# A pre-norm linear-attention and FFN block rewritten as one ordered list of operations

## The chip, the core and the metric

The kernel runs on one core of a Trainium2 chip. TensorE (PE) multiplies matrices out of SBUF into the eight banks of PSUM, VectorE (DVE) and ScalarE (ACT) work on vectors, GpSimd (POOL) builds masks, and SyncE (SP) issues the DMAs. The metric is the time of one execution on the device in microseconds (us); smaller is better.

## The reference

The sequence has 2048 rows of 512, the attention 32 heads of 16, the FFN 1792 columns in the middle. All arrays are bf16; B_x is not used.

```python
x = A_x
h = x + _A_ref(_layernorm(x), A_wqkv, A_wo)
h2 = h + _B_ref(_layernorm(h), B_w1, B_w2)

# _A_ref: q, k, v = split heads of x @ wqkv
phi = lambda t: where(t > 0, t + 1, exp(t)) + 1e-6
kv = einsum("bhsd,bhse->bhde", phi(k), v);  z = sum over s of phi(k)
o = (phi(q) @ kv) / (phi(q) . z + 1e-6);    return o @ wo
# _B_ref: return maximum(x @ w1, 0) @ w2
```

## The kernel before

The rows are 16 tiles of 128, in four chunks of four tiles. The value projection is never made for single rows: the kernel sums `gps`, the product of the normalized rows (transposed) with phi(k), over all tiles, and multiplies by the weights of v afterwards (`kvps`), masks the blocks of the heads (`kvbd`), and multiplies by wo (`mps`, kept as `m_sb`). So the attention is one loop over the tiles for k, and then, for each chunk, phi(q) divided by its denominator (`pqs`) times `m_sb`.

Stage one, for each tile t: the statistics of LN1 on DVE (`A_S`: bn_stats into `st`, bn_aggr into `mv`), its rstd by Ln and Exp on ACT, the norm on DVE (`A_N`, into `ln`), four transposes on PE and a copy out by ACT (`A_T`, into `lnT`), the k projection (`A_K`, `kps`), phi by ACT and DVE (`phi_act`, `phi_dve`, into `pk_all`) and the sum into `gps` (`A_G`). phi takes an Exp on ACT (`e`), for some tiles a Relu on ACT (`r`), then on DVE the minimum with 1 (line 211) and either an add (215) or relu and add in one (217).

Between that and the FFN stand z (`zps`), the q projections (`q_mm`, `qps`), the denominators, and h. For the first chunk PE adds x into h with an identity matrix (`h_first`, line 468) and transposes LN2's result; for the other chunks DVE adds x (line 447), and four DMA transposes issued by SP (line 456) bring LN2's result `hn` into `lnT`. LN2's norm subtracts the mean and multiplies by rstd, so it waits for rstd.

The FFN of a chunk is 14 groups `proj_group` (`pps`, four matmuls each, relu alternately by ACT, line 484, and DVE, line 486, into `at`), then four tiles of `ffn_group` (`fps`, 14 matmuls each), whose results `ffn_out` adds to h on DVE (line 501) and SP stores. The groups of the next chunk's denominators and h are woven among the first twelve projections.

The order on each engine is the order in which the program issues its instructions; `after` and `tick` put some DVE work back by a group. PSUM has two pools of four buffers, `mm` and `acc`, and a group waits for the buffer that comes next. SP issues all DMAs in one queue, and an instruction that waits there holds back all that stand behind it.

Of the kernel before, what the change touches and what calls it, by code (L numbers as in the profile page):

```python
# [14 lines left out]

@with_exitstack
def kernel(
# [10 lines left out]

# [27 lines left out]
    wqkv_v = A_wqkv.rearrange("(k p) n -> p k n", p=P)  # L56

# [45 lines left out]
    zeros = const.tile([P, CW], BF16, name="zeros")  # L103
    ident = const.tile([P, P], BF16, name="ident")
    mask = const.tile([P, P], BF16, name="mask")
    nc.vector.memset(zeros[:], 0.0)
    nc.vector.memset(eps5[:], 1e-5)
    nc.vector.memset(eps6[:], 1e-6)
    nc.vector.memset(ones[:], 1.0)
# [40 lines left out]
    hnT_c = lnT_c  # L150
    pqT_c = [big.tile([P, KD, CW], BF16, name=f"pqT{c}") for c in range(NCH)]
# [6 lines left out]
    pk_all = big.tile([P, NT, D], BF16, name="pk_all", tag="at0")  # L158

    gps = [psum.tile([P, D], F32, name=f"gps{kd}", tag="acc") for kd in range(KD)]  # L160


    def warm(n):
        for _ in range(n):
            nc.tensor.matmul(gps[3][:], lhsT=zeros[:, 0:P], rhs=zeros[:], start=True, stop=True)

    warm(9)


    def rstd_of(mv, n):  # L170
        rstd = work.tile([P, n], F32, name="rstd", tag=f"rstd{n}", bufs=4)
        nc.scalar.activation(out=rstd[:], in_=mv[:, :, 1], func=ACT.Ln, bias=eps5[:], scale=1.0)
        nc.scalar.activation(out=rstd[:], in_=rstd[:], func=ACT.Exp, scale=-0.5)
        return rstd

    def stats(mv, k, src):
        st = work.tile([P, nc.vector.BN_STATS_DIM], F32, name="st", tag="st", bufs=4)
        nc.vector.bn_stats(out=st[:], in_=src)  # L178
        nc.vector.bn_aggr(out=mv[:, k, :], in_=st[:])  # L179

    def norm(dst, src, mv, rstd, k):
        nc.vector.tensor_scalar(  # L182
            out=dst, in0=src, scalar1=mv[:, k, 0:1], scalar2=rstd[:, k : k + 1],
            op0=ALU.subtract, op1=ALU.mult,
        )

    def transpose(src, tag="mm"):
        tp = psum.tile([P, KD * P], BF16, name="tp", tag=tag)
        for kd in range(KD):
            nc.tensor.transpose(tp[:, kd * P : (kd + 1) * P], src[:, kd * P : (kd + 1) * P], ident[:])  # L190
        return tp

    def evac_T(dst3, tp, on_act, k=KD):
        src3 = tp.rearrange("p (k n) -> p k n", k=k)
        if on_act:
            nc.scalar.activation(out=dst3, in_=src3, func=ACT.Copy)  # L196
        else:
            nc.vector.tensor_copy(out=dst3, in_=src3)

    def phi_act(ps, relu_on_act):  # L200
        e = work.tile([P, CW], BF16, name="e", tag="e", bufs=4)
        nc.scalar.activation(out=e[:], in_=ps, func=ACT.Exp)  # L202
        r = None
        if relu_on_act:
            r = work.tile([P, CW], BF16, name="r", tag="r", bufs=4)
            nc.scalar.activation(out=r[:], in_=ps, func=ACT.Relu)
        return e, r

    def phi_dve(ps, dst, er):
        e, r = er  # L210
        nc.vector.tensor_scalar(  # L211
            out=e[:], in0=e[:], scalar1=1.0, scalar2=1e-6, op0=ALU.min, op1=ALU.add
        )
        if r is not None:
            nc.vector.tensor_tensor(out=dst, in0=r[:], in1=e[:], op=ALU.add)
        else:
            nc.vector.scalar_tensor_tensor(  # L217
                out=dst, in0=ps, scalar=0.0, in1=e[:], op0=ALU.max, op1=ALU.add
            )

    def q_mm(c, jq):
        qps = psum.tile([P, CW], F32, name="qps", tag="mm")
        for kd in range(KD):
            nc.tensor.matmul(  # L224
                qps[:], lhsT=wq_sb[:, kd, jq * P : (jq + 1) * P], rhs=lnT_c[c][:, kd, :],
                start=(kd == 0), stop=(kd == KD - 1),
            )
        return qps


    later = []

    def after(n, fn):
        later.append([n, fn])

    def tick():
        due = [x for x in later if x[0] <= 0]
        later[:] = [x for x in later if x[0] > 0]
        for x in later:
# [12 lines left out]


    group_of = {0: [0], 1: [1], 2: [2], 3: [3]}
    for t in range(4, NT, 2):
        group_of[t + 1] = [t, t + 1]
    where = {t: (g, k) for g in group_of.values() for k, t in enumerate(g)}
    mvs, rstds, lns, tps, kpss, ers = {}, {}, {}, {}, {}, {}

    def A_S(t):  # L260
        g, k = where[t]
        if k == 0:
            mvs[g[0]] = work.tile(
                [P, len(g), nc.vector.BN_AGGR_DIM], F32, name="mv", tag=f"mv{len(g)}", bufs=4
            )
        stats(mvs[g[0]], k, x_nat[:, t, :])
        if k == len(g) - 1:
            rstds[g[0]] = rstd_of(mvs[g[0]], len(g))
# [344 lines left out]
```

## Time and profile before

| what | value |
|---|---|
| median of 3 runs | 181.35 us (181.35 to 181.62) |
| the profiled execution | 181.33 us |
| its span | 179.6 us |
| granted TensorE clock | 0.997 |
| PE, DVE, ACT busy in the span | 170.1, 110.3, 80.9 us |
| moved by DMA | 11.69 MB, mean 65 GB/s |

The span is the time between the first and the last recorded event of the program on the core; the 1.7 us beside it are what the execution takes around it. In the rows that follow, a group is named by its line, engine and operation, what it writes and what it reads, then the number of instructions, their busy time and the mean of one in ns. PEld is the loading of weights, which overlaps PE.

### The profile page before, as it was taken

How to read it: one execution, taken by the hardware profiler on the slowest of the kernel's cores; microseconds unless marked ns; L12 is line 12 of the kernel's file. 1: busy time of each engine (PE TensorE's matmuls, PEld its weight loads, DVE VectorE, ACT ScalarE, POOL GpSimd, SP SyncE). 2: the span in 40 equal slices, each digit the busy share in tenths (PEclk: the TensorE clock that was granted, in tenths of full speed). 3: DMA queues.
4: the chain of work that ended last, by engine and by line, in shares of the span. 5: the costliest groups of instructions: out<-in, count | busy, mean ns of one | idle time of the engine just before them, and what ended most of it. 6: DMA issues, size and time to landing. Idle time of an engine off the chain costs nothing.

```text
span 179.6 us, 2419 instructions
## 1 busy us (share of the span) xinstructions
PE 170.1 (95%) x899; PEld 79.7 (44%) x916; DVE 110.3 (61%) x247; ACT 80.9 (45%) x162; POOL 4.7 (3%) x21
## 2 busy tenths in 40 slices
PE   7888999999998899999999999999999999999991
PEld 2334555546444444444444444444444444444461
DVE  4889999556898866988132788323498613343320
ACT  3868888856874997322008722003932100331000
POOL 7300000000000000000000000000000000000000
PEclk9999999999999999999999999999999999999998
DMA  5999960000000000003400000431000250000011
GB/s 135 318 346 384 374 201 2 0 0 4 0 4 0 0 0 0 2 4 70 106 29 29 0 4 0 88 89 57 0 0 4 48 127 29 29 0 4 29 58 31
DMA packets 15627, 11.69 MB, mean 65 GB/s; under 512 B 7040, under 2 KB 15104, under 8 KB 15616
## 3 DMA queue, kind: packets, MB, share of 16 engines
q1 hardware_dynamic: 15616, 11.54, 21.3%
q8 instruction: 7, 0.11, 0.3%
q14 instruction: 4, 0.03, 0.1%
HBM read 7.86 MB, written 2.10 MB: 55 GB/s over the span
## 4 chain that ended last, share of the span: by engine, by line
PE 70%; DVE 18%; ACT 6%; issue 2%; DMA 1%; DVEq 0%
PE fps L493 22%; PE pps L479 20%; PE gps L304 7%; PE kps L297 6%; DVE st L178 5%; PE qps L224 5%; PE hps L423 5%; DVE at L486 2%; PE fpsh L493 2%; DVE hn L182 2%; DVE mv L179 2%; DVE h_nat L447 1%; ACT lden L410 1%; ACT rden L412 1%; PE tp L190 1%
## 5 line engine op out<-in xcount | busy, mean ns | idle before, releaser
L479 PE MATMUL pps<-lnT,w_sb 128*128 128x512 bf16 x220 | 53.0, 379 | 0.9 <-ACT lnT L196 0.4
L493 PE MATMUL fps<-w_sb,at 128*128 128x512 bf16 x205 | 46.1, 379 | 0.6 <-DVE at L486 0.4
L484 ACT ACTIVATE at<-pps 128x512 bf16<-128x512 f32 x28 | 16.7, 595 | 60.6 <-PE pps L479 60.6
L493 PEld LDWEIGHTS <-at 128*128 128x128 bf16 x238 | 23.1, 98 | 26.2 <-DVE at L486 1.3
L479 PEld LDWEIGHTS <-w_sb 128*128 128x128 bf16 x224 | 21.9, 98 | 27.3 <-issue 1.7
L501 DVE TENSOR_TENSOR o_t<-fps,h_nat 128x512 bf16<-128x512 f32 x15 | 10.4, 692 | 29.1 <-PE fps L493 29.1
L486 DVE TENSOR_SCALAR at<-pps 128x512 bf16<-128x512 f32 x28 | 19.1, 680 | 9.3 <-PE pps L479 9.3
L304 PE MATMUL gps<-pk_all,ln 128*128 128x512 bf16 x61 | 15.9, 379 | 0.9 <-DVE pk_all L217 0.5
L423 PE MATMUL hps<-m_sb,pqs 128*128 128x512 bf16 x63 | 16.6, 379 | 0.1
L297 PE MATMUL kps<-wk_sb,lnT 128*128 128x512 bf16 x62 | 16.2, 379 | 0.1
L224 PE MATMUL qps<-lnT,wq_sb 128*128 128x512 bf16 x62 | 15.7, 379 | 0.2
L178 DVE BATCH_NORM_STATS2 st<-x_nat 128x6 f32<-128x512 bf16 x16 | 11.0, 685 | 1.7 <-DMA x_nat<-in_A_x_dram 1.7
L211 DVE TENSOR_SCALAR e<-e 128x512 bf16<-128x512 bf16 x32 | 8.9, 278 | 4.7 <-ACT e L202 4.7
L202 ACT ACTIVATE e<-qps 128x512 bf16<-128x512 f32 x16 | 9.4, 600 | 4.6 <-PE qps L224 4.6
L178 DVE BATCH_NORM_STATS2 st<-h_nat 128x6 f32<-128x512 bf16 x16 | 11.0, 689 | 0.4
L414 DVE TENSOR_TENSOR pqs<-pqT,rden 128x512 bf16<-128x512 bf16 x12 | 5.1, 425 | 9.1 <-ACT rden L412 9.0
L202 ACT ACTIVATE e<-kps 128x512 bf16<-128x512 f32 x16 | 9.5, 596 | 2.5 <-PE kps L297 2.5
L196 ACT ACTIVATE lnT<-tp 128x512 bf16<-128x512 bf16 x17 | 10.0, 590 | 0.5 <-PE tp L190 0.5
L423 PEld LDWEIGHTS <-pqs 128*128 128x128 bf16 x64 | 6.3, 98 | 8.6 <-DVE pqs L414 1.2
L304 PEld LDWEIGHTS <-ln 128*128 128x128 bf16 x64 | 6.2, 97 | 8.4 <-issue 1.3
L224 PEld LDWEIGHTS <-wq_sb 128*128 128x128 bf16 x64 | 6.0, 98 | 7.2 <-issue 0.8
L447 DVE TENSOR_TENSOR h_nat<-hps,x_nat 128x512 bf16<-128x512 f32 x12 | 8.2, 686 | 0.9 <-PE hps L423 0.8
(72 smaller groups left out, 134.8 us busy)
## 6 DMA issues: line engine op xcount, KB each, us to landing
w_sb<-in_B_w_dram SPq DMA_DIRECT2D x2, 1792.0 KB, 14.2
out_dram<-o_t SPq DMA_DIRECT2D x15, 128.0 KB, 1.7
x_nat<-in_A_x_dram SPq DMA_DIRECT2D x2, 512.0 KB, 6.5
x_nat<-in_A_x_dram SPq DMA_DIRECT2D x4, 128.0 KB, 2.2
wk_sb<-in_A_wqkv_dram SPq DMA_DIRECT2D x2, 256.0 KB, 3.3
x_nat<-in_A_x_dram SPq DMA_DIRECT2D x2, 256.0 KB, 4.3
wq_sb<-in_A_wqkv_dram SPq DMA_DIRECT2D x1, 512.0 KB, 7.9
wv_sb<-in_A_wqkv_dram SPq DMA_DIRECT2D x1, 512.0 KB, 8.9
```

Of the source, the lines that this page charges most:

```text
L178: nc.vector.bn_stats(out=st[:], in_=src)
L196: nc.scalar.activation(out=dst3, in_=src3, func=ACT.Copy)
L202: nc.scalar.activation(out=e[:], in_=ps, func=ACT.Exp)
L224: nc.tensor.matmul(qps[:], lhsT=wq_sb[:, kd, jq * P : (jq + 1) * P], rhs=lnT_c[c][:, kd, :], start=(kd == 0), stop=(kd == KD - 1),)
L297: nc.tensor.matmul(kpss[t][:], lhsT=lnT_c[c][:, kd, j * P : (j + 1) * P], rhs=wk_sb[:, kd, :], start=(kd == 0), stop=(kd == KD - 1),)
L304: nc.tensor.matmul(gps[kd][:], lhsT=lns[t][:, kd * P : (kd + 1) * P], rhs=pk_all[:, t, :], start=(t == 0), stop=(t == NT - 1),)
L423: nc.tensor.matmul(hps[:], lhsT=pqss[c][jb][:, j * P : (j + 1) * P], rhs=m_sb[:, jb, :], start=(jb == 0), stop=(jb == KD - 1 and c > 0),)
L479: nc.tensor.matmul(pps[:], lhsT=w1_sb[:, kd, f * P : (f + 1) * P], rhs=hnT_c[c][:, kd, :], start=(kd == 0), stop=(kd == KD - 1),)
L484: nc.scalar.activation(out=acts[c][:, f, :], in_=pps[:], func=ACT.Relu)
L486: nc.vector.tensor_scalar(out=acts[c][:, f, :], in0=pps[:], scalar1=0.0, scalar2=None, op0=ALU.max)
L493: nc.tensor.matmul(fps[:], lhsT=acts[c][:, f, j * P : (j + 1) * P], rhs=w2_sb[:, f, n0:n1], start=(f == 0), stop=(f == KF - 1),)
L501: nc.vector.tensor_tensor(out=o_t[:], in0=fps[:], in1=h_nat[:, t, n0:n1], op=ALU.add)
```

## The change

The pools, `after`, `tick` and `woven` are gone. Every operation is a small function, and a table ORDER lists them in the order in which they are issued; a word is a function's name and its numbers. Upper-case letters are LN1 and k: S and A the statistics of a tile, R its rstd, N the norm, T and E (or V, on DVE) a transpose on PE and the copy out, X the transpose by DMA, K the projection, F, U, M, D the Exp, Relu, minimum and add of phi, G the sum. Lower-case ones are LN2 and the FFN: h, hD, s, a, r, n, t, e, v, x, then p (projection), pA and pD (relu on ACT or DVE), f, fo and fd. Q, qF, qU, qM, qD are the q projection and its phi, d, dl, dx, dm the denominators, lx to lo the loads. The last number of p, Q, K, h, f is the bank of PSUM, which is now one tile `bk` of eight banks; F, U, M, D, their q forms, pA, pD, gA, mA, mD and rm take a tile number and a count, and with a count of 2 they handle two banks (1024 columns) in one instruction. Tiles 0 to 3 have phi one by one.

Six things change in what is computed where. Tiles 8 to 15 of LN1 are transposed by DMA (X). The Relu of every phi is on ACT. In the first chunk DVE adds x to h (hD), and the ident matmul is gone. LN2's n only subtracts the mean; rstd, which is positive and passes through the relu, is multiplied in by fo, so n no longer waits for rstd. The loads of wq, wv, wo, w1 and w2 are in halves, in another order. LN1's rows lie in `h_nat`, and pk(t) in `pk_lo` and `acts[0]`.

```diff
+ORDER = """
+lx.0.1 lx.1.1 lx.2.1 lk.0.2 lk.2.2 lx.3.1 lx.4.2 lx.6.2 lx.8.4 lx.12.4 table const masks warm.9.7 S.0 S.1 A.0
+R.0.1 A.1 S.2 R.1.1 N.0.0.2 N.0.2.2 A.2 N.1 S.3 A.3 T.0.3.2.2 T.0.0.0.2 E.0.0.2 E.0.2.2 T.1.1 warm.1.7 E.1
...
-    lnT_c = [big.tile([P, KD, CW], BF16, name=f"lnT{c}") for c in range(NCH)]
+    ln_nat = h_nat
+    bk = psum.tile([P, 8, CW], F32, name="bk")
+    op_X = lambda t: nc.sync.dma_start_transpose(out=lnT_of(t), in_=ln_nat[:, t, :])
+    op_x = lambda t: nc.sync.dma_start_transpose(out=lnT_of(t), in_=hn[:, t % NQ, :])
...
+    def relu_of(kind, i, n):
+        nc.scalar.activation(out=buf(rb, kind, i, n), in_=bank(at_bank[kind, i], n), func=ACT.Relu)
+    def add_of(kind, i, n):
+        nc.vector.tensor_tensor(
+            out=dsts[kind](i, n), in0=buf(rb, kind, i, n), in1=buf(eb, kind, i, n), op=ALU.add
+        )
...
-        norm(hns[c, j][:], h_nat[:, c * CT + j, :], mv2[c, j0], rstd2[c, j0], j - j0)
+    def op_n(t):
+        nc.vector.tensor_scalar(
+            out=hn[:, t % NQ, :], in0=h_nat[:, t, :], scalar1=mv2[:, t, 0:1], scalar2=None,
+            op0=ALU.subtract,
+        )
...
-        nc.tensor.matmul(hps[:], lhsT=ident[:], rhs=x_nat[:, j, :], start=False, stop=True)
-        nc.scalar.activation(out=h_nat[:, j, :], in_=hps[:], func=ACT.Copy)
+    def op_hD(t, n=1):
+        nc.vector.tensor_tensor(
+            out=h_nat[:, t : t + n, :], in0=bank(at_bank["h", t], n), in1=x_nat[:, t : t + n, :],
+            op=ALU.add,
+        )
+    def op_pD(c, f, n):
+        nc.vector.tensor_scalar(
+            out=acts[c % 2][:, f : f + n, :], in0=bank(at_bank["p", c, f], n),
+            scalar1=0.0, scalar2=None, op0=ALU.max,
+        )
...
-        nc.vector.tensor_tensor(out=o_t[:], in0=fps[:], in1=h_nat[:, t, n0:n1], op=ALU.add)
-        nc.sync.dma_start(out=of_v[:, t, n0:n1], in_=o_t[:])
+    def op_fo(t, k=0, w=KD):
+        cols = slice(k * P, (k + w) * P)
+        nc.vector.scalar_tensor_tensor(
+            out=o_t[:, t % NO, cols], in0=bk[:, at_bank["f", t, k], 0 : w * P],
+            scalar=rstd2[:, t : t + 1], in1=h_nat[:, t, cols], op0=ALU.mult, op1=ALU.add,
+        )
...
+    for word in ORDER.split():
+        name, *idx = word.split(".")
+        ops[name](*map(int, idx))
```

The first place is SP's queue during LN1, after the loads of the first eight tiles. Before:

```order
L76 DMA x_nat<-in_A_x_dram 128x4x512 x2
L93 DMA wq_sb<-in_A_wqkv_dram 128x4x512
L94 DMA wv_sb<-in_A_wqkv_dram 128x4x512
L95 DMA wo_sb<-in_A_wo_dram 128x4x512
L96 DMA w_sb<-in_B_w_dram 128x4x1792
L97 DMA w_sb<-in_B_w_dram 128x14x512
```

Changed (lnT_83 and lnT_84 are the third and fourth chunk, h_nat holds LN1's rows, w_sb is w1 or w2):

```order
L198 DMA x_nat<-in_A_x_dram 128x4x512 x2
L201 DMA wv_sb<-in_A_wqkv_dram 128x2x512 x2
L201 DMA wq_sb<-in_A_wqkv_dram 128x2x512
L201 DMA w_sb<-in_B_w_dram 128x2x1792
L269 DMA_TRANSPOSE lnT_83<-h_nat 128x4x128 x4
L269 DMA_TRANSPOSE lnT_84<-h_nat 128x4x128 x2
L201 DMA wq_sb<-in_A_wqkv_dram 128x2x512
L269 DMA_TRANSPOSE lnT_84<-h_nat 128x4x128 x2
L201 DMA w_sb<-in_B_w_dram 128x7x512
L201 DMA wo_sb<-in_A_wo_dram 128x2x512
```

The transposes, each of which waits for its tile's norm on DVE, now stand ahead of half of wq, of wo and of most of the FFN weights.

The second place is DVE from kvbd to LN2 of the first chunk. Before (pqT_128 and pqT_129 are phi(q) of the first and second chunk):

```order
L367 TENSOR_TENSOR kvbd<-kvps,mask 128x512
L211 TENSOR_SCALAR e<-e 128x512
L215 TENSOR_TENSOR pqT_129<-r,e 128x512
L386 CAST m_sb<-mps 128x512 x2
L403 TENSOR_TENSOR pqs<-rps,pqT_128 128x512 x4
L211 TENSOR_SCALAR e<-e 128x512
L215 TENSOR_TENSOR pqT_129<-r,e 128x512
L211 TENSOR_SCALAR e<-e 128x512
L217 SCALAR_TENSOR_TENSOR pqT_129<-qps,e 128x512
```

Changed (pqT_85 and pqT_86 are the same two, bk is PSUM):

```order
L370 TENSOR_TENSOR kvbd<-bk,mask 128x512
L302 TENSOR_SCALAR eb<-eb 128x1024
L380 CAST m_sb<-bk 128x1024
L305 TENSOR_TENSOR pqT_86<-rb,eb 128x1024
L408 TENSOR_TENSOR pqs<-bk,pqT_85 128x1024 x2
L441 TENSOR_TENSOR h_nat<-bk,x_nat 128x512 x2
L217 BN_STATS st_101<-h_nat 128x6 x2
L218 BN_AGGR mv_102<-st_101 128x2
L441 TENSOR_TENSOR h_nat<-bk,x_nat 128x512
L236 TENSOR_SCALAR hn<-h_nat,mv_102 128x512
```

Pairs stand in place of single instructions, h of the first chunk comes to DVE, and the rest of the second chunk's phi moves behind LN2's statistics.

The third place is DVE in the FFN's projections of the second chunk, while h and LN2 of the third are made. Before:

```order
L486 TENSOR_SCALAR at<-pps 128x512
L447 TENSOR_TENSOR h_nat<-hps,x_nat 128x512
L178 BN_STATS st<-h_nat 128x6
L179 BN_AGGR mv_1293<-st 128x2
L182 TENSOR_SCALAR hn<-h_nat,mv_1293,rstd 128x512 x4
L486 TENSOR_SCALAR at<-pps 128x512
L501 TENSOR_TENSOR o_t<-fps,h_nat 128x512 x4
```

Changed (at_96 is the second chunk's buffer):

```order
L305 TENSOR_TENSOR pqT_88<-rb,eb 128x1024
L236 TENSOR_SCALAR hn<-h_nat,mv_102 128x512
L217 BN_STATS st_101<-h_nat 128x6
L218 BN_AGGR mv_102<-st_101 128x2 x2
L236 TENSOR_SCALAR hn<-h_nat,mv_102 128x512 x2
L218 BN_AGGR mv_102<-st_101 128x2
L236 TENSOR_SCALAR hn<-h_nat,mv_102 128x512
L461 TENSOR_SCALAR at_96<-bk 128x1024
L478 SCALAR_TENSOR_TENSOR gT<-bk,rstd_103,h_nat 128x512
```

Each norm follows its own tile's statistics instead of all four standing behind the chunk's rstd, and the last relu of the chunk is one instruction for two groups.

More of the change, by code (lines that the diff above doesn't have):

```diff
@@ L16 @@
+"""
 @with_exitstack
@@ L176, in stats @@
[L176 to L181, printed above, removed]
+    acts = [big.tile([P, KF, CW], BF16, name=f"at{i}") for i in range(2)]
+    pk_lo = big.tile([P, 2, D], BF16, name="pk_lo")
+    st = big.tile([P, NT, nc.vector.BN_STATS_DIM], F32, name="st")
+    mv = big.tile([P, NT, nc.vector.BN_AGGR_DIM], F32, name="mv")
@@ L254 @@
[L254 to L268, printed above, removed]
@@ L379 @@
-    rd4 = work.tile([P, CW], BF16, name="rd4", tag="rd4", bufs=1)
-    nc.scalar.activation(out=rd4[:], in_=ld4[:], func=ACT.Exp, scale=-1.0)
-    q11 = q_mm(1, 1)
-    for jb in range(KD):
-        mps = psum.tile([P, D], F32, name="mps", tag="acc")
-        nc.tensor.matmul(mps[:], lhsT=kvbd[:, jb, :], rhs=wo_sb[:, jb, :], start=True, stop=True)
-        if jb < 2:
-            nc.vector.tensor_copy(out=m_sb[:, jb, :], in_=mps[:])
-        else:
-            nc.scalar.activation(out=m_sb[:, jb, :], in_=mps[:], func=ACT.Copy)
@@ L389 @@
-    er11 = phi_act(q11[:], True)
-    pqss = [[None] * KD for _ in range(NCH)]
-    def new_pqs(c, jb):
-        pqss[c][jb] = work.tile([P, CW], BF16, name="pqs", tag="pqs", bufs=8)
-        return pqss[c][jb]
-    rpss = [psum.tile([P, CW], F32, name="rps", tag="mm" if jb < 2 else "acc") for jb in range(KD)]
-    for jb in range(KD):
-        rows = slice(jb * Q4, (jb + 1) * Q4)
-        nc.tensor.matmul(rpss[jb][:], lhsT=erep[rows, :], rhs=rd4[rows, :], start=True, stop=True)
-    for jb in range(KD):
-        pqs = new_pqs(0, jb)
-        nc.vector.tensor_tensor(out=pqs[:], in0=rpss[jb][:], in1=pqT_c[0][:, jb, :], op=ALU.mult)
@@ L418, with op_kx, op_m, op_mA @@
-    mv2, rstd2, hns = {}, {}, {}
-    def h_mm(c, j):
-        hps = psum.tile([P, D], F32, name="hps", tag="acc")
+    def op_kx():
+        kvps = bk[:, at_bank["kv"], :].rearrange("p (k n) -> p k n", k=KD)
+        nc.vector.tensor_tensor(out=kvbd[:], in0=kvps, in1=mask_b, op=ALU.mult)
+    def op_m(jb, b):
+        at_bank["m", jb] = b
+        nc.tensor.matmul(bk[:, b, :], lhsT=kvbd[:, jb, :], rhs=wo_sb[:, jb, :], start=True, stop=True)
+    def op_mA(jb, n):
+        nc.scalar.activation(out=m_sb[:, jb : jb + n, :], in_=bank(at_bank["m", jb], n), func=ACT.Copy)
@@ L422, in h_mm, with op_mD, op_d4 @@
+    def op_mD(jb, n):
+        nc.vector.tensor_copy(out=m_sb[:, jb : jb + n, :], in_=bank(at_bank["m", jb], n))
+    def op_d4(c, b):
+        at_bank["d4", c] = b
         for jb in range(KD):
             nc.tensor.matmul(
[L424 to L435 removed]
@@ L471, with op_dl4 @@
-    acts = {}
-    def proj_group(c, f):
-        if f == 0:
-            pool = big if c % 2 == 0 else work
-            acts[c] = pool.tile([P, KF, CW], BF16, name="at", tag=f"at{c % 2}", bufs=1)
-        pps = psum.tile([P, CW], F32, name="pps", tag="acc" if c == 0 and f < 4 else "mm")
+                bk[jb * Q4 : (jb + 1) * Q4, b, :], lhsT=zhd[:, jb, :], rhs=pqT[c][:, jb, :],
+                start=True, stop=True,
+            )
+    def op_dl4(c):
+        nc.scalar.activation(
+            out=ld[:, c % 2, :], in_=bk[:, at_bank["d4", c], :], func=ACT.Ln, bias=eps6[:], scale=1.0
+        )
@@ new lines, in op_dx4, with op_rp, op_rm @@
+    def op_dx4(c):
+        nc.scalar.activation(out=rd[:, c % 2, :], in_=ld[:, c % 2, :], func=ACT.Exp, scale=-1.0)
+    def op_rp(c, jb, b):
+        at_bank["rp", c, jb] = b
+        rows = slice(jb * Q4, (jb + 1) * Q4)
+        nc.tensor.matmul(
+            bk[:, b, :], lhsT=erep[rows, :], rhs=rd[rows, c % 2, :], start=True, stop=True
+        )
+    def op_rm(c, jb, n):
+        i = (c * KD + jb) % NQ
+        nc.vector.tensor_tensor(
+            out=pqs[:, i : i + n, :], in0=bank(at_bank["rp", c, jb], n), in1=pqT[c][:, jb : jb + n, :],
+            op=ALU.mult,
+        )
```

569 lines of the change are left out of this document (229 added, 340 removed).

## The prediction

> **What bounds the kernel now.** I read the page's busy shares first, then the busy time by stage, then the chain that ended last.
>
> ```profile
> span 179.6 us, 2419 instructions
> PE 170.1 (95%) x899; PEld 79.7 (44%) x916; DVE 110.3 (61%) x247; ACT 80.9 (45%) x162; POOL 4.7 (3%) x21
> GB/s 135 318 346 384 374 201 2 0 0 4 0 4 0 0 0 0 2 4 70 106 29 29 0 4 0 88 89 57 0 0 4 48 127 29 29 0 4 29 58 31
> ```
>
> PE is busy almost throughout, but a busy PE is not a full PE, so I cut the span into four stages at places where the chain changes hands (start:end, length, PE, PEld, DVE, ACT, POOL busy, granted clock, DMA share, GB/s).
>
> ```profile
> 0.00:14.47 14.47, 11.04 (x53) 4.56 (x55) 10.18 (x31) 9.27 (x23) 4.71 (x21) 1.00 0.88 272
> 14.47:47.70 33.23, 32.99 (x253) 17.66 (x257) 26.04 (x69) 25.84 (x54) 0.00 (x0) 1.00 0.34 120
> 47.70:61.12 13.42, 12.35 (x67) 5.38 (x68) 12.24 (x31) 9.42 (x21) 0.00 (x0) 1.00 0.00 1
> 61.12:176.03 114.91, 113.70 (x528) 52.11 (x537) 61.46 (x119) 36.39 (x67) 0.00 (x0) 1.00 0.12 32
> ```
>
> The chain in order of time gives the price of each kind of work when it follows its like without a gap (start, length, what).
>
> ```profile
> 2.90 0.70 DVE st L178
> ...
> 4.78 0.85 DVE ln L182 x2
> 5.63 0.61 DVE st L178
> ...
> 8.10 0.18 DVE mv L179
> 8.28 0.19 DVE e L211
> 8.56 0.43 DVE pk_all L215
> 8.99 0.35 DVE ln L182
> ...
> 14.47 1.02 PE gps L304 x4
> 15.50 0.22 PE tp L190 x4
> 15.72 0.86 PE kps L297 x4
> ...
> 41.29 1.58 PE zps L340 x64
> ...
> 45.48 0.89 PE kvps L362 x16
> 46.37 0.36 PE d L373 x4
> ...
> 49.24 2.39 DVE pqs L403 x4
> ...
> 59.11 0.49 ACT r L206
> ...
> 61.12 1.89 PE pps L479 x8
> ...
> 93.51 1.73 PE pps L479 x8
> ...
> 172.93 3.07 PE fpsh L493 x28
> 176.02 0.42 DVE o_t L501
> ```
>
> Eight 512-column matmuls cost 1.73, so one costs 0.216 and a group of four 0.865; a transpose of one tile (four pieces) 0.22; zps 1.58; kvps 0.89; d 0.36. By count the kernel has 728 matmuls of 512 columns (64 each of kps, gps, qps and hps, 4 with ident, 4 mps, 4 rps, 12 dps, 224 pps, 224 fps with the halves counted together) and 20 tile transposes: 157.4 + 4.4 + 1.58 + 0.89 + 0.36 = 164.7 us that PE must spend. Its last matmul ends at 176.0, so 11.3 us are lost to waits and the cold start. By stage: up to 14.47 PE has done 24 matmuls and five transposes, 6.3 us, and lost 8.2. From 14.47 to 47.70 it lost 0.3. From 47.70 to 61.12 the work is 12.1 and 1.3 is lost, while DVE is busy 12.24 of 13.42. From 61.12 on the work is 524 x 0.216 = 113.3 of 114.9: 1.6 lost. Thus a gain can come from fewer PE instructions, from the start, from the DVE stage, and hardly from anything else.
>
> **PE work removed.** Tiles 8 to 15 of LN1 are no longer transposed on PE: 8 x 0.22 = 1.76. The four ident matmuls that added x into h are gone: 4 x 0.216 = 0.86. PE is the bound where they stood, so 2.62 us fall out whole, to 162.1. Rows of the trace behind the remaining prices:
>
> ```profile
> L501 DVE TENSOR_TENSOR o_t<-fps,h_nat 128x512 bf16<-128x512 f32 x15 | 10.4, 692 | 29.1 <-PE fps L493 29.1
> L501 DVE TENSOR_TENSOR o_t<-fpsh,h_nat 128x256 bf16<-128x256 f32 x2 | 0.8, 424 | 1.9 <-PE fpsh L493 1.9
> L196 ACT ACTIVATE lnT<-tp 128x512 bf16<-128x512 bf16 x17 | 10.0, 590 | 0.5 <-PE tp L190 0.5
> L196 ACT ACTIVATE lnT<-tph 128x256 bf16<-128x256 bf16 x2 | 0.7, 384 | 0.1
> 81.13 5.23 SPq L456 DMA_TRANSPOSE lnT<-hn  x4
> lnT<-hn SPq DMA_TRANSPOSE x12, 2.4
> x_nat<-in_A_x_dram SPq DMA_DIRECT2D x2, 512.0 KB, 6.5
> wk_sb<-in_A_wqkv_dram SPq DMA_DIRECT2D x2, 256.0 KB, 3.3
> ```
>
> **Pairs.** 256 columns more cost DVE 268 ns, so 512 more cost 0.54; one f32 instruction after another costs 0.60 (2.39 for four), a pair 1.14 instead of 1.20. On ACT 256 more cost 206 ns, 512 more 0.41: a pair 0.90 instead of 0.98. No 1024-column row exists; the bounds are 0.60 (nothing for the second half, excluded by the slope) and 1.20 on DVE. So pairing gives each engine about 7% on these instructions, and the first half waits for the second group, 0.865 us. It is not on the path while PE is the bound. The work on ACT also falls by eight evacuations of 0.49, and rises because all feature-map relus are now there.
>
> **The start.** PE's first rows of work (the warm-up matmuls, then K.0 and K.1):
>
> ```profile
> 1.24 3.63 PE L165 MATMUL gps<-zeros 128*128 128x512 bf16 x9 [1.24 <-DVE ones L109]
> 5.92 1.03 PE L297 MATMUL kps<-wk_sb,lnT 128*128 128x512 bf16 x4
> 7.75 1.03 PE L297 MATMUL kps<-wk_sb,lnT 128*128 128x512 bf16 x4
> ```
>
> DVE now does S.0, S.1, A.0, A.1, S.2 before N.0: 2.90 + 0.70 + 0.61 + 0.18 + 0.18 + 0.61 = 5.2, two halves of N.0 to 5.7, transposes, two half evacuations on ACT, and K.0 at about 6.7, 0.8 later than its 5.9 before; K.1 then follows at once where it used to come 1.8 later. DVE feeds the rest: sixteen S, A, N at 0.61 + 0.18 + 0.35, four M and D alone (0.62), three pairs (about 0.96, my estimate between 0.62 and 1.24), the copy V.2 as 0.43: 24.0 from 2.9, with some 0.4 of waits N.15 ends at 27.3. PE from K.0 up to K.15 has fifteen K, eleven G, six transposes, 23.8 us, with some 1.5 of short waits on T.3, G.1 and G.4: K.15's turn is at 32.0. Nine more groups, 7.8, and Q.0.3 ends at 39.8.
>
> The moved transposes run beside this. SP spends 1.31 on each (5.23 for four). X.10 leaves when N.10 is done (21.65 by the same count), then X.11, X.13, X.12, the half of wq (0.5) and X.14: X.15 is issued at 28.7 and lands 2.4 later, 31.1, 0.9 ahead of its use. The loads that stood in front of them are out of the way: 4.2 MB by about 15 us at the GB/s row (40 slices of 4.49 us). Queued behind them: half of wq, issued at 27.4, needed at 32.9 (256 KB landed in 3.3); wo, needed about 45; w2 and half of w1, needed from 61: 3.2 MB at 350 GB/s after 30 is 39. Four more load issues cost SP some 0.5 each, covered by that slack. If the cover were gone, each us of lateness of X.15 is a us of the end.
>
> **The middle.** From Q.0.3's end at 39.8 to the first FFN matmul there are G.15, zps, twelve Q groups, kvps, four m, d4, four rp, sixteen h, four transposes and four d: 21.0 us. I followed the order by the prices above. The path is kx, m, then d4, its Ln and Exp on ACT, rp, the two paired products: h.0 waits 0.4 for the second. DVE then does hD, s, a, n for four tiles and the pair q.1.2; the last transposes and d.1.3 wait 0.45 for n.2 and v.3. LN2 no longer waits for rstd in front of n, which is applied in fo. So 0.85 is lost where stages two and three lost 1.6, and p.0.0 starts at 61.7. Start and middle together lose 8.6 instead of 9.7: -1.1. By then PE has done four Q groups and four d more than before at its 61.12, 4.33 us.
>
> **The FFN.** Its lost 1.6 is mostly the order on DVE (start, length, engine, line; in brackets the idle time and what ended it):
>
> ```profile
> 112.44 0.69 DVE L486 TENSOR_SCALAR at<-pps 128x512 bf16<-128x512 f32 x1
> 113.19 2.98 PE L493 MATMUL fps<-w_sb,at 128*128 128x512 bf16 x12 [0.18 <-DVE at L486]
> DVE hn L182 <- ACT rstd L173: 2.4, 4, 0.6
> ```
>
> The relu of the last group stands behind four hn, which wait for rstd. In the new order the n need no rstd and the last relus stand clear of them. A pair of banks is free 1.2 after its second group and is wanted again 1.73 after: 0.5 of slack each. In the second chunk I find n.9 ending 5.5 us ahead of p.2.3; its transpose, fourth on SP, lands 1.1 ahead. The outputs fd.0 to fd.2 now queue behind four transposes on SP; fo.4, which reuses their buffer, comes 2 to 3 us after they land. Half the loss stays, by my choice, because those margins are thin: -0.8. The tail is as it was: two halves of 256 columns, one DVE instruction of 0.42, one output.
>
> [...]
>
> **Sum.** The profiled execution took 181.33 (span 179.6 and 1.7 around it; the median is 181.35). 181.33 - 2.62 - 1.1 - 0.8 = 176.8; I add 0.2 for semaphore latencies that I left out: 177.0.
>
> **Rivals.**
> 1. Only the removed work pays: the new waits eat what the old ones cost. 181.33 - 2.62 = 178.7, 178.0 to 179.5. For it: margins of 0.4 to 1.1 at six places. Against it: DVE's path is shorter at each.
> 2. More comes out: the start has 8 us of loss and the middle 0.85, and PE catches up to the X bound (31.1 instead of 32.0) while the FFN loses nothing: 177.0 - 0.9 - 0.8 = 175.3, about 175.2 to 176.1.
> 3. The DMA path is late, which is the one that can end slower. Eight transposes now feed K.8 to K.15 and SP is busy with them from 22 to 30. Each landed in 2.4 with the engines idle; 512 KB behind other loads took 6.5. At 6.5 X.15 lands at 35.2, 3.2 after its turn: 180.2. Past 7.7 from issue to landing the kernel is slower than before, about 182. Against it: the loads are in by 15.
> 4. The start runs at half speed. By the three PE rows quoted for the start, the nine warm-up matmuls went at 0.40 each, the four of K.0 and of K.1 at 0.22. With K.0 0.8 later and only transposes in front, eight to sixteen matmuls could run at 0.40, 1.5 to 3 us of which DVE's pace hides about half: 178.5. [...]
>
> **Chances.** The forecast (176.1 to 178.0) 0.56; rival 1 0.20; rival 2 0.12; rival 3 0.06, of which 0.04 ends slower; rival 4 0.06. From 175.4 to 179.3 some 0.1 is left out. Faster by over 0.2% (about what a measurement here can tell from no change) 0.94, within it 0.02, slower 0.04.
>
> **What would show it.** Right: 48 transposes on PE, no ident matmul in h; X.15 landed before K.15; p.0.0 (line 450) starting near 61.7; pps and fps with under 1 us of waits. The sum is wrong if PE waits for lnT from a DMA in LN1, if matmuls near 7 us take 0.40, if a 1024-column instruction costs well over 1.14 on DVE, or if PE waits for a bank of a pair.

## The result and the profile after

The changed kernel took 176.24 us (median of 4 runs, 175.64 to 177.9) against 181.43 for the kernel before, run beside it: a ratio of 0.973, with a 95% interval of 0.966 to 0.980. Four more runs in a later round gave 175.94 (175.62 to 176.23) and 0.970 (0.968 to 0.971). The profiled execution took 175.64, with a span of 173.9. One execution of a variant further down was disturbed (258.56 us at a mean clock of 0.661) and enters no ratio.

After the change, the page's busy shares, the engines' shares of the chain that ended last, and two of the costliest groups:

```profile
span 173.9 us, 2279 instructions
PE 166.9 (96%) x865; PEld 78.0 (45%) x880; DVE 104.0 (60%) x210; ACT 71.4 (41%) x112; POOL 4.8 (3%) x21
...
PE 92%; DMA 2%; DVE 2%; SPq 1%; issue 1%
...
L461 DVE TENSOR_SCALAR at<-bk 128x1024 bf16<-128x1024 f32 x18 | 22.0, 1222 | 20.1 <-PE bk L450 19.9
L456 ACT ACTIVATE at<-bk 128x1024 bf16<-128x1024 f32 x10 | 10.1, 1023 | 45.7 <-PE bk L450 45.7
```

A pair lasts 1222 ns on DVE and 1023 on ACT, each counted by itself. What it costs in a queue is less, because the next instruction starts before it has ended: 1.14 on DVE, by the two starts below, and 0.90 to 0.92 on ACT (as in the chains of the experiments), where two singles cost 1.20 and 0.98.

```profile
47.50 1.23 DVE L380 CAST m_sb<-bk 128x1024 bf16<-128x1024 f32 x1 [0.80 <-PE bk L374]
48.64 0.68 DVE L305 TENSOR_TENSOR pqT<-rb,eb 128x1024 bf16<-128x1024 bf16 x1
```

The busy time by stage, cut behind m (48.85), at the first FFN matmul (62.09) and at the end of the last matmul (170.93); columns as before:

```profile
0.00:14.47 14.47, 11.24 (x57) 4.80 (x59) 10.35 (x34) 9.24 (x23) 4.75 (x21) 1.00 0.84 266
14.47:48.85 34.38, 34.16 (x231) 16.55 (x232) 20.96 (x52) 24.66 (x37) 0.00 (x0) 1.00 0.51 149
48.85:62.09 13.24, 13.13 (x72) 6.13 (x74) 11.06 (x23) 9.84 (x12) 0.00 (x0) 1.00 0.00 1
62.09:170.93 108.84, 108.34 (x510) 50.49 (x516) 61.17 (x102) 27.62 (x44) 0.00 (x0) 1.00 0.13 33
```

The third stage begins later in the work than the one before did, which was cut ahead of m. From the start of m (46.43) to the first FFN matmul DVE is busy 12.68 of 15.66 us and PE 15.52; before it was 12.24 of 13.42 and 12.35. So DVE has as much to do as before, but PE has more beside it, the four Q groups and four d that came forward, and DVE no longer sets the pace. In the last, 504 matmuls of 0.216 are 108.9 us of work, and the stage lasts 108.84: nothing is lost there any more, where 1.7 of 114.91 was. The waits of PE over the whole program (engine, line, what it waited for: us in total, times, longest), three of seven from before, then all from after:

```profile
PE tp L190 <- DVE hn L182: 0.6, 1, 0.6
...
PE pps L479 <- ACT lnT L196: 0.4, 1, 0.4
PE fps L493 <- DVE at L486: 0.4, 2, 0.2
```

```profile
PE bk L248 <- DVE h_nat L229: 1.8, 2, 1.4
PE bk L212 <- DVE ones L174: 1.3, 1, 1.3
```

Of the seven before, those for hn, lnT and at lay in the middle and the FFN. The two that are left lie in the first 10 us. The chain after, in order of time (start, length, what):

```profile
3.18 4.20 DMA x_nat<-in_A_x_dram
...
7.40 0.70 DVE st L215
...
9.85 0.41 PE bk L248 x4
...
62.09 8.63 PE bk L450 x40
...
161.81 9.12 PE bk L470 x56
...
170.95 0.48 DVE gT L478
```

From 9.85 to the last output the chain runs through PE, but for one copy by DVE at 10.28. Ahead of that stands a load: the statistics of tile 3 wait for rows that were issued at 3.18 and landed at 7.37, and PE idles until 9.85. SP's queue in LN1:

```profile
16.59 9.93 SPq L269 DMA_TRANSPOSE lnT<-h_nat  x6
...
27.24 2.53 SPq L269 DMA_TRANSPOSE lnT<-h_nat  x2
```

The last transpose is issued by 29.77, and in this execution no matmul of LN1 waits for one.

So, counted stage by stage, the 5.7 us of span lie in four places: 2.62 of PE work removed; 0.74 less lost up to the first FFN matmul (it starts 0.97 later, with 4.33 more work moved ahead of it and 2.62 taken out); 1.74 less lost in the FFN (114.91 - 108.84 - 4.33); and 0.6 from the end of the last matmul to the end of the span (3.57, then 2.97).

### The profile page after: what moved, and what is told of

The parts are those of the page before. It is cut to its first block, busy times and chain, and to the rows that moved or that the text cites. A ratio compares the mean times of both kernels' runs of the same rounds, so it can differ in the third digit from the quotient of the medians.

```text
span 173.9 us, 2279 instructions
## 1 busy us (share of the span) xinstructions
PE 166.9 (96%) x865; PEld 78.0 (45%) x880; DVE 104.0 (60%) x210; ACT 71.4 (41%) x112; POOL 4.8 (3%) x21
## 4 chain that ended last, share of the span: by engine, by line
PE 92%; DMA 2%; DVE 2%; SPq 1%; issue 1%
PE bk L470 28%; PE bk L450 28%; PE bk L285 8%; PE bk L435 8%; PE bk L329 8%; PE bk L277 7%; DMA x_nat<-in_A_x_dram 2%; PE bk L415 1%; PE bk L248 1%; DVE st L215 1%; PE bk L337 1%; SPq L198 1%; PE bk L374 1%; SPq L201 1%; PE bk L362 1%
## 5 line engine op out<-in xcount | busy, mean ns | idle before, releaser
L450 PE MATMUL bk<-lnT,w_sb 128*128 128x512 bf16 x218 | 51.5, 379 | 0.3
L470 PE MATMUL bk<-w_sb,at 128*128 128x512 bf16 (+1 forms) x236 | 50.7, 366 | 0.1
L461 DVE TENSOR_SCALAR at<-bk 128x1024 bf16<-128x1024 f32 x18 | 22.0, 1222 | 20.1 <-PE bk L450 19.9
L450 PEld LDWEIGHTS <-w_sb 128*128 128x128 bf16 x224 | 21.9, 98 | 26.4
L456 ACT ACTIVATE at<-bk 128x1024 bf16<-128x1024 f32 x10 | 10.1, 1023 | 45.7 <-PE bk L450 45.7
L478 DVE SCALAR_TENSOR_TENSOR gT<-bk,rstd,h_nat 128x512 bf16<-128x512 f32 (+1 forms) x17 | 12.0, 718 | 20.0 <-PE bk L470 19.9
L295 ACT ACTIVATE eb<-bk 128x1024 bf16<-128x1024 f32 (+1 forms) x18 | 16.7, 926 | 8.1 <-PE bk L285 5.8
L298 ACT ACTIVATE rb<-bk 128x1024 bf16<-128x1024 f32 (+1 forms) x18 | 16.6, 928 | 2.8 <-PE bk L277 1.5
L285 PE MATMUL bk<-lnT,wq_sb 128*128 128x512 bf16 x60 | 15.1, 379 | 0.3
L277 PE MATMUL bk<-wk_sb,lnT 128*128 128x512 bf16 x63 | 15.3, 380 | 0.1
L435 PE MATMUL bk<-m_sb,pqs 128*128 128x512 bf16 x63 | 15.2, 379 | 0.1
L329 PE MATMUL bk<-at,h_nat 128*128 128x512 bf16 x56 | 13.6, 379 | 0.1
```

Of the source, the lines that this page charges most:

```text
L277: nc.tensor.matmul(bk[:, b, :], lhsT=lnT[c][:, kd, j * P : (j + 1) * P], rhs=wk_sb[:, kd, :], start=(kd == 0), stop=(kd == KD - 1),)
L285: nc.tensor.matmul(bk[:, b, :], lhsT=wq_sb[:, kd, j * P : (j + 1) * P], rhs=lnT[c][:, kd, :], start=(kd == 0), stop=(kd == KD - 1),)
L295: nc.scalar.activation(out=buf(eb, kind, i, n), in_=bank(at_bank[kind, i], n), func=ACT.Exp)
L298: nc.scalar.activation(out=buf(rb, kind, i, n), in_=bank(at_bank[kind, i], n), func=ACT.Relu)
L329: nc.tensor.matmul(bk[:, KD + kd, :], lhsT=ln_nat[:, t, kd * P : (kd + 1) * P], rhs=pk(t)[:, 0, :], start=(t == 0), stop=(t == NT - 1),)
L435: nc.tensor.matmul(bk[:, b, :], lhsT=pqs[:, (c * KD + jb) % NQ, j * P : (j + 1) * P], rhs=m_sb[:, jb, :], start=(jb == 0), stop=(jb == KD ...
```

## The experiments

The theory was that the shorter waits of the new order pay beside the removed work; the rival, that the removed work pays alone. Four parts of the change (the transposes by DMA, rstd out of the norm, no ident matmul, the pairs) were undone in the new list, and three parts were tried alone in the kernel before. The kernel before stood at 181.44 to 181.48 in all of them. "After" is the changed kernel's later median, 175.94; it ran beside three of the variants only (the transposes and the rstd alone in the kernel before, and the first of the start), so elsewhere a difference from it under some 0.5 us says little. A variant's line numbers differ from the changed kernel's by a few.

**The transposes by DMA, undone.** Tiles 8 to 15 go back to PE and ACT. The variant ran twice; the trace is of the second time.

```diff
-X.9 X.8 X.10 X.11 R.12.2 K.9.1 G.4 K.8.0 G.5
+T.9.1 T.8.0 G.4 E.9 E.8 K.9.1 T.10.2 K.8.0 T.11.3 R.12.2 E.10 E.11 G.5
-X.13 X.12 lq.0.2 X.14 X.15
+lq.0.2
```

> The changed kernel with LN1's tiles 8 to 15 transposed on PE and copied out by ACT again (32 transposes, 8 copies), the rest as it is. Theory (PE is full there, so its work sets the time): 8 x 0.22 = 1.8 us slower than the changed kernel, 177.4 against its profiled 175.6, the FFN unchanged. Rival A (the moved transposes hardly pay, since SP's queue and the landing cost PE what they save): within 0.5 us of it. Rival B (the copies on ACT hold PE up as well): 3 us or more slower.

> The changed kernel with LN1's tiles 8 to 15 transposed on PE again, a second time for a profile by stage: its time was 179.2, 3.2 us more than the changed kernel's 176.0, where the work of 32 transposes is 1.76. Theory (the rest is waits of the copies on ACT, which stand in front of or behind 1 us pairs): up to the end of Q.0.3 PE loses 1 to 1.5 us more than in the changed kernel, in gaps in front of K.8 to K.15. Rival (transposes cost PE more than 0.22 a tile there): no more gaps, but longer transposes.

Measured: 179.18 (0.987, interval 0.986 to 0.989) and 179.14 (0.986, 0.984 to 0.988), 3.2 over after, where the transposes are 1.76: rival B of the first expectation, and the gap ahead of K that the second one expected. The longer of two new waits of PE (the other is 0.2, for banks behind a phi), and the chain ahead of it:

```profile
PE bk L276 <- ACT lnT L257: 1.2, 1, 1.2
```

```profile
20.40 1.02 ACT eb L294
21.42 0.91 ACT rb L297
22.34 0.50 ACT lnT L257
...
22.88 1.04 PE bk L276 x4
```

The copy of a transposed tile (lnT) queues on ACT behind an Exp and a Relu of a pair, 1.93 us, and PE's next K waits for it. 1.76 + 1.4 is the 3.2: a transpose on PE cost its copy's place on ACT too. The copies were tried at one place in the list only.

**The transposes by DMA, alone in the kernel before.**

```diff
+        if t >= 8:
+            nc.sync.dma_start_transpose(out=lnT_c[c][:, :, j * P : (j + 1) * P], in_=lns[t][:])
-        if ok(i + 1):
+        if ok(i + 1) and i + 1 < 8:
             A_T(i + 1)
...   (the loads of wo, w1 and w2 go behind them)
```

> The kernel before with one part of the change alone: LN1's tiles 8 to 15 go to lnT by DMA transposes issued right after their norm, and the loads of wo, w1 and w2 stand behind them in SP's queue. Theory (the removed PE work pays wherever the transposes are not late): 32 transposes fewer, -1.76, 179.6 against 181.4. Rival A (without the new order PE waits for the landing, some 2.5 us after a norm that comes two tiles ahead): 181 or more. Rival B (ACT, relieved of eight copies, speeds the start up too): 178.5 or less.

Measured: 180.43 (0.995, 0.993 to 0.996), 1.0 less than before, between the theory and rival A. The trace, of a run of 180.70, shows that little of it is the removed work: zps starts at 41.17 instead of 41.29, the last matmul ends at 175.85 instead of 176.02, and another 0.42 lies behind it (3.15 to the end instead of 3.57, see the last section). What left PE came back as waits, first for a chain through ACT and DVE (22.6 to 26.4), then for transposes that were issued too late for their K (PEld's waits for them are 2.4 in seven):

```profile
PEld L297 <- DMA lnT<-ln: 2.4, 7, 0.6
```

```profile
32.43 2.47 DMA lnT<-ln
...
34.95 1.04 PE kps L297 x4
```

So in the old order another chain in LN1 was about as long as PE's work. The new order starts the norms earlier and does not wait there; no other order was run.

**The loads ahead of the transposes.** The list after, with all weight loads issued ahead of X.9.

```diff
-lv.0.2 lq.2.2 l1.2.2 X.9 X.8 X.10 X.11
+lv.0.2 lq.2.2 l1.2.2 lq.0.2 l2.7.7 lo.0.2 l2.0.7 lo.2.2 l1.0.2 X.9 X.8 X.10 X.11
```

> The changed kernel with all weight loads ahead of LN1's DMA transposes in SP's queue (the place that they had before). Theory (a transpose that is issued into queues full of loads lands after them): the loads are 8.4 MB, done at about 25 us, so X.9, issued at 16.6, lands near 25 instead of 21 and K.9 waits some 3 us; 2 to 4 us slower than the changed kernel. Rival A (a transpose lands in about 2.5 us whatever else moves): within 0.5 us, and the order of the loads did not matter.

Measured: 185.29 (1.019, 1.016 to 1.022), 9.3 over after, and more than expected. In the trace K.9 waits for its transpose, which lands 9.4 us after its issue, behind the loads, where the median in the changed kernel is 2.5. PE's wait, the chain, and the busy time behind the gap:

```profile
PE bk L276 <- DMA lnT<-h_nat: 7.7, 1, 7.7
```

```profile
18.64 9.38 DMA lnT<-h_nat
...
28.06 1.89 PE bk L276 x4
```

```profile
28.00:33.00 5.00, 4.89 (x13) 1.83 (x15) 0.00 (x0) 0.02 (x1) 0.00 (x0) 0.56 0.47 93
```

After 7.7 us without a matmul, four matmuls take 1.89 instead of 0.86: PE's clock in the five us is 0.56. So 7.7 of wait and about 2 of slow matmuls make the 9.3 (p.0.0 starts 9.7 later). The theory of a late landing holds, with a price more than twice the most it said, and so does the mechanism of the prediction's rival 3; the order of SP's queue is what kept it away.

**rstd back in the norm.** The list after, with rstd made tile by tile behind its statistics and multiplied into n, and a plain add in fo.

```diff
-            scalar1=mv2[:, t, 0:1], scalar2=None, op0=ALU.subtract,
+            scalar1=mv2[:, t, 0:1], scalar2=rstd2[:, t : t + 1], op0=ALU.subtract, op1=ALU.mult,
...
-a.1 hD.3 n.1 t.1.5
+a.1 r.1.1 hD.3 n.1 t.1.5
```

> The changed kernel with LN2's rstd back in the norm n (per tile, Ln and Exp on ACT right after its statistics) and out of fo, which adds only. Theory (the wait for rstd stands in the chain only in the middle, where four n in a row feed PE's transposes; in the FFN there is slack of about 1 us): 1 to 2 us slower, all of it between the q projections and the first FFN projection. Rival A (it cost and costs nothing): within 0.3 us. Rival B (it was what emptied the FFN of waits): the FFN's lost time goes from 0 back to about 1.6 us.

Measured: 180.91 (median of 12, 180.41 to 182.54; ratio 0.999, 0.997 to 1.002), 5.0 over after: nearly the whole gain of the change is gone. The trace is of a run of 182.37; p.0.0 starts at 67.33, 5.2 later, and 1.9 of this is there at kvps already. In the middle the chain leaves PE:

```profile
57.94 1.02 ACT eb L295
58.97 0.92 ACT rb L298
59.88 0.19 ACT rstd L221
...
60.33 0.42 DVE hn L236
```

rstd queues on ACT behind the phi of another chunk, which costs 3.3 in the middle, and the FFN loses 1.6 (110.4 for 108.9 of work), with the same chain ahead of its transposes: theory and rival B are both right in part, and 3.3 + 1.6 is the 5.0. The 1.9 are the start, at half clock in this run (below, on the hardware). The variant also makes rstd tile by tile, with 60 instructions on ACT in the FFN instead of 44, so this price is not that of the wait alone.

**rstd out of the norm, alone in the kernel before.**

```diff
-        norm(hns[c, j][:], h_nat[:, c * CT + j, :], mv2[c, j0], rstd2[c, j0], j - j0)
+        nc.vector.tensor_scalar(out=hns[c, j][:], in0=h_nat[:, c * CT + j, :],
+            scalar1=mv2[c, j0][:, j - j0, 0:1], scalar2=None, op0=ALU.subtract)
...   (o_t = fps * rstd + h in one scalar_tensor_tensor)
```

> The kernel before with another part alone: LN2's norm subtracts the mean only, and rstd is multiplied in with the last addition, so that hn no longer waits for rstd. Putting rstd back into the changed kernel cost about 4.7 us, 3.2 of it in the middle and 1.5 in the FFN. Theory (in the old order DVE's own queue is the limit in the middle, and the wait for rstd is 2.4 in four waits): 0.7 to 1.5 us faster, 180 to 180.7, half in the middle and half in the FFN. Rival A (it is worth 3 us or more in any order): 178.5 or less. Rival B (it pays only with the new order): 181.2 or more.

Measured: 180.71 (0.996, 0.995 to 0.997), 0.7 less. The first FFN matmul starts at 61.06 as before (61.12), so the middle gained nothing, and the FFN takes 114.16 instead of 114.91. The size was forecast, its half in the middle was not: there rstd still stands on ACT ahead of a phi and the copies of the last transposes.

**The ident matmuls back.** The list after, with x added into the first chunk's h by PE and copied out by ACT.

```diff
-h.2.6 qF.2.2.2 qU.2.2.2 hD.0 hD.1 s.1 s.0 a.1 hD.3
+h.2.6 qF.2.2.2 qU.2.2.2 hA.0 hA.1 s.1 s.0 a.1 hA.3
```

> The changed kernel with the four ident matmuls back: in the first chunk PE adds x into h and ACT copies h out, where DVE added x. Theory (PE's work, 4 x 0.216, is paid, and ACT, which has pairs of 1 us in its queue, is later than DVE was): 0.9 to 1.6 us slower than the changed kernel. Rival (DVE is the bound of this stage, and four adds of 0.6 fewer shorten it): the same or up to 1 us faster.

Measured: 181.99 (median of 12, 180.38 to 185.41; 1.002, 1.000 to 1.004), 6 over after, and far beyond the 0.9 to 1.6 that the theory had. The chain around it:

```profile
56.45 1.02 ACT eb L294
57.48 0.91 ACT rb L297
58.39 0.99 ACT h_nat L442 x2
...
59.40 1.29 DVE st L216 x2
...
60.81 0.36 DVE hn L235
...
61.22 0.61 PE bk L247 x4
61.83 3.67 PE bk L284 x12
```

The copies stand on ACT behind the Exp and the Relu of a pair, which wait for their own projection until 56.43; PE waits 3.72 for the norm, and the twelve matmuls after that take 3.67 instead of 2.59. 0.86 + 3.7 + 1.1, and 0.4 for the slow transposes, less 0.25 that PE was ahead at kvps, is the 5.8 by which p.0.0 is later (67.90). Copies ahead of that pair were not tried.

**The ident matmuls away, alone in the kernel before.**

```diff
-        nc.tensor.matmul(hps[:], lhsT=ident[:], rhs=x_nat[:, j, :], start=False, stop=True)
-        nc.scalar.activation(out=h_nat[:, j, :], in_=hps[:], func=ACT.Copy)
+        nc.vector.tensor_tensor(out=h_nat[:, j, :], in0=hps[:], in1=x_nat[:, j, :], op=ALU.add)
```

> The kernel before with this part alone: no ident matmul, DVE adds x to h of the first chunk. Theory (in the old order DVE is busy 12.2 of 13.4 us there and sets the pace, so four adds of 0.6 more than cancel 0.86 of PE work): 1.2 to 2.4 us slower than before, 182.6 to 183.8. Rival (PE's work counts here too): 0.5 to 0.9 us faster.

Measured: 184.81 (1.020, 1.017 to 1.023), 3.3 slower though PE has 0.86 less to do, and more than forecast. DVE was what the middle waited for, and it got four additions more. PE's rows (start, length, what; idle time before) and the window behind the gap:

```profile
59.41 0.40 PE L190 MATMUL tp<-ident,hn 128*128 128x128 bf16 x4 [3.82 <-DVE hn L182]
59.65 1.67 PE L224 MATMUL qps<-lnT,wq_sb 128*128 128x512 bf16 x4
```

```profile
59.40:63.00 3.60, 3.59 (x16) 1.78 (x17) 2.79 (x8) 2.44 (x6) 0.00 (x0) 0.57 0.00 0
```

The gap of 3.82 us is followed by a clock of 0.57: DVE's delay is paid as a wait and again as slow matmuls, which the forecast had left out.

**Pairs split.** The list after, with every operation on two tiles issued as two.

```diff
+        if name in PAIRS and n == 2:
+            ops[name](*at, 1)
+            at[-1] += 1
+            ops[name](*at, 1)
```

> The changed kernel with every paired instruction (feature map, FFN relus, copies of g, m and rm) replaced by two of 512 columns at the same place in the order. Theory (pairs save 0.06 on DVE and 0.08 on ACT each and are off the path while PE is full): within 0.5 us of the changed kernel, and FFN waits below 0.3 us. Rival A (the pairs are a main source of the gain): 1.5 us or more slower. Rival B (pairs hold banks too long, singles free the first bank earlier): 0.5 us or more faster.

Measured: 175.97 (175.38 to 176.46; 0.969, 0.967 to 0.971), the same as after, as the theory said. DVE's relus, 18 of 1222 ns in pairs, are 36 of 685 in singles:

```profile
L464 DVE TENSOR_SCALAR at<-bk 128x512 bf16<-128x512 f32 x36 | 23.4, 685 | 17.9 <-PE bk L453 15.8 <-ACT rb L301 2.0
```

The 1.4 us that pairs save DVE there lie in its idle time.

**The start.** Two variants of the loads: tile 3's rows ahead of the second half of wk, with tile 2's work pulled forward; and wk issued by ACT.

```diff
-lk.0.2 lk.2.2 lx.3.1
+lk.0.2 lx.3.1 lk.2.2
```

> The changed kernel with the start mended: x tile 3 is loaded ahead of the second half of wk, rstd of tiles 2 and 3 is taken apart, and norm, transpose and copy of tile 2 stand ahead of the statistics of tile 3 and later. Theory (in the trace DVE waits 1.4 us for x tile 3, and PE stands still from 8.4 to 9.85, which in some runs also drops its clock for some 3 us, as the run with rstd in n shows at 12 us): 0.5 to 1.2 us faster than the changed kernel, 175.0 or less, and all runs within 0.4%. Rival (DVE's total up to N.15 sets the pace whatever its order): within 0.3 us of the changed kernel.

```diff
-    op_lk = lambda k, n: load_d(wk_sb, wqkv_v[:, :, D : 2 * D], k, n)
+    op_lk = lambda k, n: nc.scalar.dma_start(
+        out=wk_sb[:, k : k + n, :], in_=wqkv_v[:, k : k + n, D : 2 * D]
+    )
```

> The changed kernel with the two loads of wk issued by ACT ahead of its table load, so that SP issues the x tiles 0 to 7 without them in between (each issue takes SP 0.4 to 0.5). Theory (the start waits for the arrival of x tile 3, issued at 3.18 and landed at 7.4, and the queues run below 320 GB/s in the first 4.4 us because the issues come one after the other): x tile 3 lands near 6.5 and the kernel is 0.4 to 1.0 us faster than the changed kernel, 175.0 to 175.6. Rival A (the bytes set the start, in whatever order and from whatever queue, as the run with tile 3 moved forward suggests): within 0.3 us. Rival B (x tile 0 shares the queues with wk and lands later): 0.3 us or more slower.

Measured: 176.26 (0.971, 0.970 to 0.972) and 177.03 (0.974, 0.971 to 0.976): both theories failed, the first variant is as fast as after, the second about 1 us slower (rival B). In the first, the wait went to the next load, tiles 4 and 5:

```profile
3.65 6.21 DMA x_nat<-in_A_x_dram
```

In the second, the first tiles took longer to land beside wk's loads (3.4 from issue to landing, the median of the first four, instead of 2.4), the third tile landed at 5.75, K.0 started at 8.28, and its matmuls ran at 0.43 each, as the warm-up's do:

```profile
7.03 1.03 PE L249 MATMUL bk<-ident,h_nat 128*128 128x128 bf16 x8 [1.76 <-DVE h_nat L230]
...
8.28 2.90 PE L278 MATMUL bk<-wk_sb,lnT 128*128 128x512 bf16 x8
```

In both, the start still waits for a load, only for another one.

**The changed kernel again**, beside these.

> The changed kernel unchanged, beside the others. Theory: 175.6 to 176.3, with single runs near 178 where the clock falls at the start. Rival (its four runs were spread by something else): no run with a clock below 0.995 is longer than the rest.

Measured: 175.94, as the theory said; no run had a clock below 0.995, so its explanation of the run of 177.9 was not put to the test. The profiled run, 176.23, differs from the other of 175.64 ahead of the FFN alone: tile 3's rows land at 7.73 instead of 7.37, a K of LN1 waits 0.23 for its DMA transpose at 22.77, and p.0.0 starts at 62.69 instead of 62.09; the FFN takes 108.83. So the transposes' margin is nearly nothing at that place.

No variant had a lower median than the changed kernel.

## Why the prediction was right

The forecast was 177.0, in the range 175.4 to 179.3; the median is 176.24 and 175.94. That it came out so near is in part luck, since the terms missed in both directions. Its own steps:

- **PE work removed, 2.62.** Right, by the count: no ident matmul, 48 transposes on PE. But the experiments show that this work pays only with the order: alone, the DMA transposes brought 1.0, of which the trace shows 0.2 ahead of the last matmul's end, and the removal of ident lost 3.3. The prediction's reason, that PE was the bound where they stood, was too simple: in LN1 and in the middle the chains through ACT and DVE were nearly as long as PE's work. The new list has these chains shorter, and there the work falls out.
- **Start and middle, 1.1.** Measured 0.74. K.0 came at 6.52 (6.7 said), N.15 at 27.1 (27.3), X.15 was out at 29.77 (30.0). Q.0.3 ended at 40.48 instead of 39.8. The missed term is the landing of tile 3 at 7.37: I had taken the loads as in time for DVE, "some 0.4 of waits", where this one alone is 1.4 of DVE's time, and PE's wait behind it is 1.4 too. The middle took 21.6 of 21.0 work, better than the 21.9 said.
- **FFN, half of the 1.6.** Measured: all of it, 1.7. I kept half because margins of 0.5 to 1.1 looked thin; in the trace none was crossed. The size of the term was wrong, its mechanism right as far as it was tried: with rstd out of n, the kernel before loses 0.75 less and its wait for the last relu (`at`) is gone; with rstd back in n, the FFN of the new list loses 1.6 again, more of it ahead of the DMA transposes than of the relu.
- **Pairs, nothing on the path.** Right: split, they make no difference. They hold up no bank either: of PE's seven kinds of wait before and its two after, none is for a bank. The prices were right too: 1.14 on DVE and 0.90 on ACT were forecast as the time until the next instruction, and 1.14 and 0.90 to 0.92 were measured; the 1222 and 1023 ns are the lengths of one instruction, which the forecast did not price.
- **The tail, unchanged, and 0.2 of latencies.** The tail is 0.6 shorter, which I did not foresee; the 0.2 was an estimate of mine that no run shows by itself, and the latencies are in the stages' sums above.

The terms thus missed by 0.36, -0.94, -0.6 and -0.2, together -1.38; the profiled 175.64 is 1.36 from 177.0. **Rival 1** is refuted: 178.7 would need the waits unchanged. **Rival 2** had the FFN right and the start wrong; its range of 175.2 to 176.1 holds five of the eight runs, but not for its reason: PE did not catch up with X's bound, and the tail gave what the start did not. **Rival 3** did not happen, but for 0.23 of wait for a transpose in the second profile; loads ahead of the transposes bring it about; its price, one us of the end for each us of lateness, left out the slow matmuls behind the gap. **Rival 4** did not happen in the first profile of the changed kernel, where K.0 and K.1 ran at full speed (eight matmuls in 1.90 us), but it did where wk was issued by ACT (2.90). The run of 177.9 had a mean clock of 0.990, and the rstd variant's profile shows that one stretch of 3.4 us at half clock makes 0.991; that fits such a stretch, but no trace tells where it was.

What stays open: the sum of the three parts alone is +1.6 (-1.0, -0.7, +3.3), the whole is -5.5, and undoing them in the new list costs 3.2, 5.0 and 6.0. So the order and the parts pay together. The three prices add up to far more than the whole and hold for one place in the list each; at a better place an undone part might cost less. The list's order was not run with none of the parts, so what it is worth by itself has no number, and neither has the Relu of every phi on ACT nor the halving of the loads.

## What to carry to other kernels

Here, removing work from the bound engine paid only where no chain through the other engines was equally long (alone, the DMA transposes brought 1.0 of their 1.76 us, and the removal of ident lost 3.3). Before counting such work, follow that chain in the stage where the work stands, and price the queue it then lands in (a copy or a small rstd behind two 1 us instructions on ACT cost more here than the work itself: 1.4 us ahead of K, 3.3 in the middle). The gaps of 3.7 us and more on PE were paid twice, once as wait and again as half a clock (0.50 for 3.41 us or twice that), so an estimate of a late wait should hold both. Put transposes by DMA ahead of bulk loads in the queue (behind them one landed 9.4 us after its issue, where the median is 2.5 ahead of them), and undo a part in the new order as well as trying it alone in the old one: the two gave different answers for each of the three parts that were tried both ways.

## What the runs showed of the hardware

**Half a clock behind a gap.** Before its next matmul PE waited 3.72, 3.82 and 7.7 us in three variants (ident back, ident away, loads first). In their traces the granted clock is 0.50 from 60.48 to 63.89, from 59.89 to 63.30 and from 25.55 to 32.38: for 3.41 us, or twice that, and in two of the three from a moment before PE goes on (61.22 and 28.06). By windows it is 0.50 from 61.20 to 63.60, 0.57 from 59.40 to 63.00 and 0.56 from 28 to 33. But the rstd variant's start shows such a stretch, 11.94 to 15.35, after a gap of 1.47, while gaps of 1.43 and 1.5 at the same place in the two profiles of the changed kernel (mean clocks 1.000 and 0.999) did not bring it: the length of the gap does not tell by itself. Two windows, first in that variant, then in the changed kernel (the clock is the third number from the end):

```profile
9.00:12.00 3.00, 1.66 (x12) 0.86 (x13) 2.96 (x10) 2.38 (x7) 0.00 (x0) 0.99 1.06 350
12.00:15.00 3.00, 3.00 (x14) 1.61 (x13) 3.00 (x11) 1.95 (x5) 0.00 (x0) 0.50 1.00 368
```

```profile
9.00:12.00 3.00, 2.03 (x17) 1.18 (x18) 2.97 (x10) 2.83 (x8) 0.00 (x0) 1.00 1.02 312
12.00:15.00 3.00, 2.95 (x18) 1.50 (x17) 3.00 (x11) 2.88 (x7) 0.00 (x0) 1.00 1.07 391
```

Runs of that variant fall into 180.4 to 181.2 and 182.3 to 182.5, as if the loss came and went; one of the slower ones alone left a trace. What brings such a stretch was not shown. And the granted clock does not show all: in the wk variant's start that column reads 1.00 (from 0 to 9 us and from 9 to 12), while eight matmuls from 8.28 take 2.90 us, where the changed kernel's, from 6.52, take 1.90. There the durations tell.

**A packet of the instruction queue in the tail.** In 4 of the 13 undisturbed profiles a packet of the instruction queue falls behind the last matmul (before, with ident away, with rstd out, and with the transposes back on PE); from that matmul to the end they take 3.3 to 3.6 us. The other nine have no such packet and take 2.96 to 3.15. In the kernel before, from 176 to 180 us:

```profile
q14 instruction: 1, 0.01, 0.7%
```

The kernel before has it and, with its transposes by DMA, has not: 3.57 and 3.15. The changed kernel has it not and, with its transposes on PE, has: 2.97 and 3.34. So some 0.4 of the tail's 0.6 goes with the packet, by association; what sets it was not tried.
